# Both heads' scores on the two halves of the array's rows in four fp16 passes; P stays in PSUM and is transposed as two fp16 words by transfers; a new order

## The chip, the cores and the metric

The kernel runs on one core of one Trainium2 chip. The core has TensorE (PE, matrix products on an array of 128 rows by 128 columns, results in PSUM), VectorE (DVE), ScalarE (ACT), GpSimd (POOL), and SyncE (SP), which here issues all DMA transfers. SBUF is the on-chip memory that operands lie in; PSUM has eight banks of 512 fp32 columns by 128 partitions. The metric is the device time of one execution in microseconds.

## The reference

Attention with a forget decay over 8 batches, 8 heads, 576 positions and head size 64, then a layer with a softmax-gated activation (SoLU) and a layer norm on 4608 tokens:

```python
cum = np.cumsum(np.log(np.clip(f, 0.0001, 1.0)), axis=-1)
scores = scale * np.matmul(q, k.transpose(0, 1, 3, 2))
scores = np.where(causal, -1e9, scores + cum[:, :, :, None] - cum[:, :, None, :])
attn = np.exp(scores - np.max(scores, axis=-1, keepdims=True))
attn = attn / (np.sum(attn, axis=-1, keepdims=True) + 1e-09)
x = np.matmul(attn, v)              # to (4608, 512)
h = x @ w_in                        # (4608, 1024)
e = np.exp(h - np.max(h, axis=-1, keepdims=True))
solu = h * e / (np.sum(e, axis=-1, keepdims=True) + 1e-09)
ln = (solu - mean) / np.sqrt(var + 1e-06) * g_ln
out = ln @ w_out                    # (4608, 512)
```

The term cum of the query cancels in the softmax, so only that of the key is added. All is computed to about fp32 accuracy.

## The kernel before

**Words.** A number is held as a high and a low word, and a product of two such numbers is three matmuls: high by high, high by low, low by high. x, P (the softmax), v, the activation z and both weights are two fp16 words; q and k are two fp32r words.

**Tiling.** The work unit of attention is a pair of heads p (32 pairs, 4 in a batch). A pair has five query tiles i: 64, 128, 128, 128 and 128 queries against 64 + 128 i keys. Tiles 0 to 2 are half 0, tiles 3 and 4 half 1. The layer works on 36 blocks of 128 tokens, as soon as all the pairs of a batch's half are done. The names in the listings: `qs`, `ks`, `kz`, `qz` are q's and k's words stacked to 128 rows, `p` the scores and P, `pth`/`ptl` the transposed high and low words of P, `v` the words of v, `x_h`/`x_l` the attention's output, `hps` the two banks of x @ w_in, `z`/`zz` the activation and its transposed words, `ps`, `ps_t`, `ps_o` pools of two banks each.

**A pair.** `load` brings raw q and k by DMA. `split_qk` makes the high words (POOL, L589) and low words (POOL or DVE, L592) and copies them by DMA on SP into the stacked buffers (L339). `score_products` runs each head's scores as two fp32r passes on all 128 rows, L657 and L658; the second also adds the decay. Half 0 of batch 0 uses native fp32 instead (L655, values L774), which need no splitting. `scores`: DVE masks and reduces to the row's extreme, from PSUM to SBUF (L678); ACT takes exp with its sum (L681); DVE inverts the sum (L692, L693); POOL normalises in place (L708). `transposes`: PE transposes P square by square (L739) into `ps_t`, ACT takes the high word (L333), DVE the low one (L747). For i = 4, POOL and DVE make the words before (L703, L705) and two DMA transposes turn them (L342). `values`: transposed P by v, the first key tile on the whole array (L778), the others with each head on half of the array's columns (L782); ACT and DVE (L801, L802) write x's words.

**A layer.** L818 to L820 compute h; DVE L831 and ACT L834 the softmax; DVE L840 and following the gate; ACT L846 the squares; POOL L335 and DVE L860 the words of z. For layers 5 to 29 they are turned by two DMA transposes of 64 blocks; in others PE transposes z (L872). L888 to L890 multiply by w_out.

**What sets the order.** `Plan` is a list scheduler inside the kernel. Every operation has an engine, a cost, a due time (tables such as `DUE`, `EARLY`, `PAIR`, `AT_P`, `AT_L`) and what it reads, writes and takes from the pools. It fixes each engine's order; at run time each engine works through its list in that order and waits for semaphores. Where the plan has a gap on PE at the beginning and end of the program (`FILLED`), PE gets filler matmuls on an identity matrix, whose results are never used (L991).

Of the kernel before, what the change touches and what calls it, by code (L numbers as in the profile page):

```python
# [8 lines left out]
F32 = mybir.dt.float32  # L9
# [15 lines left out]
HALF_S = 320  # L25
MASK = -8.0e9
# [13 lines left out]
VN, VN_EARLY = 2 * NQ, 6  # L40
# [4 lines left out]
W_UP, W_TOP = (1, 1, 1, 1, 3, 3, 1, 1), (1, 1, 1, 1, 1, 1, 1, 1)  # L45
P_32, X_32 = (1, 1, 2, 1), (1, 2, 2, 1, 1, 2, 1, 2)
TURN = (450.0, 15.0, 1700.0)
FILLED = ((0.0, 140.0, 1.2), (690.0, 1000.0, 0.8))
TURNED = (5, 30)
Z_ENG = (3, 3, 1, 2)  # L50
# [4 lines left out]
SWITCH = ((0.0, 40.0, 0.0, 95.0), (0.0, 0.0, 0.0, 95.0), (0.0, 10.0, 0.0, 95.0), (130.0, 230.0, 180.0, 0.0))  # L55
# [11 lines left out]
class Plan:  # L67
# [31 lines left out]
    def schedule(self):  # L99
# [11 lines left out]
        for _ in self.ops:  # L111
# [79 lines left out]
DUE = dict(load=77.279, split=-5.82, upper=-59.07, v=-11.029, S=((-16.591, 2.389), (-10.866, -1.366), (-5.374, -8.943), (-5.783, 2.152), (-2.369, 2.528)), T=((-4.114,), (-6.578,), (0.027, -77.756), (12.862, 14.095), (-144.678, 29.668, 76.368)), V=((16.423, 371.464), (24.511, 165.955)))  # L191
EARLY = dict(load=-5.393, split=100.725, upper=-110.557, v=36.25, S=((216.478, -198.746), (23.491, -109.734), (23.153, -123.713), (-123.145, 60.456), (26.752, 113.365)), T=((-12.366,), (-36.759,), (-81.739, -143.07), (38.749, -11.206), (-229.138, -88.73, -36.262)), V=((-26.507, -137.733), (60.804, 84.836)))
PAIR = 23.079
C_OUT = 31.47
START = 86.666
HALF = ((64.967, -14.868), (32.745, -34.71))
W_IN = (-57.941, 54.591)
W_OUT = (103.025, 310.791)
LOAD = (198.891, -63.738)
WI_SCALE = (-43.671, -130.632)  # L200
VDUE = ((-38.21, -22.856, 38.942), (79.121, -21.859, -165.431), (55.69, -110.294, -55.795))
W_SCALE = 138.576
# [10 lines left out]
def tile_kernel(ctx: ExitStack, tc: tile.TileContext, qk, v, f, w_in, w_out, g_ln, out):  # L213

    nc = tc.nc  # L220

    def early(p, half):

        return p < NPAIR and half == 0
# [3 lines left out]
    plan = Plan(s=2, t=2, o=2)  # L228
# [34 lines left out]
    op(POOL, 1500, -85, masks, writes=[("mask",)])

    raw = [sb(f"raw_{n}", 2, S) for n in range(2)]
    hi = [sb(f"hi_{n}", S, dtype=F32R) for n in range(2)]

    def q32(n):
        return buf(f"{('qs', 'vs')[n // 2]}_{n % 2}", "q", 2, HALF_S)

    def k32(n):
        return buf(f"{('kz', 'ks')[n // 2]}_{n % 2}", "k", 2, HALF_S)

    def qs(p):
# [12 lines left out]
    def ptx(p, half, x):
        w = (64 + 256 * 5, 256 * 9)[half]
        if early(p, half):
            return buf(f"pt{'hl'[x]}_{half}", "f32", w)  # L290
        return buf(f"pt{'hl'[x]}_{half}", "f16", w, dtype=F16)

    nm = [sb(f"nm_{n}", NQ, 2) for n in range(2)]

    sums = [[sb(f"sm_{n}_{i}", 2 if i == 1 else 1, 2) for i in range(1, NQ)] for n in range(2)]
    inverses = [[sb(f"ri_{n}_{i}", 2 if i == 1 else 1, 2) for i in range(1, NQ)] for n in range(2)]
    sm, ri = ([[x[0][:, 0], x[0][:, 1], *(y[:, 0] for y in x[1:])] for x in xs] for xs in (sums, inverses))

    def epsilons():
        for t in sums[0] + sums[1]:  # L300
            nc.gpsimd.memset(t, 1.0)
    op(POOL, 1000, -70, epsilons, writes=[("eps",)])
# [43 lines left out]
    c_dram = nc.dram_tensor("c_scratch", [2 * B * H, 2, S], F32).ap()  # L346
    ft, zero = et[:B * H, :S], zt[:B * H, :S]
    cc = buf("pth_1", "cc", 256 * 9, dtype=F32R)[:B * H].rearrange("p (o r s) -> p o r s", o=2, r=2)
    nhalf = sb("nhalf", 1, p=B * H)
    dma(-99, ft, f.rearrange("b h s -> (b h) s"), 144, writes=[("e",)])  # L350
    op(DVE, 400, -99, lambda: nc.vector.memset(zero, 0.0), writes=[("z",)])

    for n, sl in enumerate((slice(0, HALF_S), slice(HALF_S, S))):
        op(DVE, (330, 300)[n], -99 + n, lambda sl=sl: nc.vector.tensor_scalar(ft[:, sl], ft[:, sl], 1.0e-4, 1.0, ALU.max, ALU.min),
           reads=[("e",)], writes=[("f", n)], port=True)
        op(ACT, (560, 490)[n], -99 + n, lambda sl=sl: nc.scalar.activation(ft[:, sl], ft[:, sl], AF.Ln), reads=[("e",)], writes=[("f", n)])

    op(ACT, 1500, -40, lambda: nc.scalar.activation(nhalf, ft[:, 0:1], AF.Exp), reads=[("e",), ("f", 0), ("f", 1)], writes=[("table",)])


    c32 = pt[4][:H, :2 * HALF_S]
    first = yt[:B * H, :HALF_S]
    op(DVE, 830, -99, lambda: nc.vector.tensor_tensor_scan(first, ft[:, :HALF_S], zero[:, :HALF_S], 0.0, ALU.add, ALU.add),
       reads=[("e",), ("f", 0), ("z",)], writes=[("y",)], port=True)
    op(DVE, 1380, -30, lambda: nc.vector.tensor_tensor_scan(zero, ft, zero, 0.0, ALU.add, ALU.add),
       reads=[("e",), ("f", 0), ("f", 1)], writes=[("z",)], port=True)
# [7 lines left out]
    summed = [("p", 4), ("p", 4, "c"), ("p", 4, "d")]

    for c in range(2):
        def zeros(t=qz[c]):
            nc.vector.memset(t.bitcast(F32), 0.0)
            nc.vector.memset(t.bitcast(F32)[D:D + 2], -8.0)
        op(DVE, 1000, -98, zeros, writes=[("qz", c, h) for h in range(2)])  # L380
# [19 lines left out]
    def weights(src, n, due, t, tk, w, wk, first=(), clear=()):  # L400
# [637 lines left out]
```

## Time and profile before

| | us |
|---|---|
| median of 3 runs | 762.63 (761.61 to 763.7) |
| span of the profiled execution, first to last instruction | 757.0 |
| mean granted TensorE clock | 0.998 |
| PE's first matmul | 3.41 |
| windows 0 to 72 us, PE busy | 65.25 |
| 72 to 200 us, PE busy | 119.14 |
| 600 to 683 us, PE busy | 79.87 |

The span is the profiled execution's own time from its first to its last instruction; the runs' times also hold what lies around it, 5.6 us by the median. Busy times of PE hold overlap, since a matmul is counted until its modelled end while the next has begun. A row of a group names the line, the engine, the operation, the tiles (out<-in), the shape and the count, then busy time and mean, then the idle time just before and what ended it. A row of a timeline begins with start and duration.

### The profile page before, as it was taken

The numbers are of one execution on the slowest core, as the hardware profiler recorded it, in microseconds if no ns is written. First come the engines' busy times: TensorE is split into PE (matmuls) and PEld (weight loads), VectorE is DVE, ScalarE is ACT, GpSimd is POOL, SyncE is SP. The second block draws the span as 40 slices with busy tenths as digits, with TensorE's granted clock in tenths as the row PEclk, the third lists the DMA queues.
The fourth block names the chain that finished last, engine by engine and source line by source line (L and its number), as shares of the span: only waits on it lengthen the run. The fifth ranks groups of instructions, "written<-read, shape, count | busy, mean of one in ns | idle before, by whom it ended". The sixth has DMA issues, their size and how long they took to land. (4 is left out here: it accounts for less than half of the span.)

```text
span 757.0 us, 15810 instructions
## 1 busy us (share of the span) xinstructions
PE 722.8 (95%) x4983; PEld 453.5 (60%) x4983; DVE 608.3 (80%) x1828; ACT 474.1 (63%) x1239; POOL 456.7 (60%) x645
## 2 busy tenths in 40 slices
PE   8998999988999999999999999999999999999998
PEld 7775676655656566555556666555565555554445
DVE  6557888899997899989599999999897869883343
ACT  5698977676665667755466677655565556653333
POOL 5537496656674787668377777775786666531220
PEclk9999999999999999999999999999999999999999
DMA  9557948968879898989789899889899788442001
GB/s 320 139 210 207 272 115 223 206 169 213 197 172 214 173 239 177 225 207 213 165 188 211 200 228 213 202 206 192 189 206 202 146 192 166 95 106 42 29 15 42
DMA packets 176851, 134.87 MB, mean 178 GB/s; under 512 B 128704, under 2 KB 139712, under 8 KB 175744
## 3 DMA queue, kind: packets, MB, share of 16 engines
q1 hardware_dynamic: 176768, 133.87, 75.3%
q8 instruction: 39, 0.64, 0.4%
q14 instruction: 44, 0.36, 0.2%
HBM read 39.51 MB, written 10.03 MB: 65 GB/s over the span
## 5 line engine op out<-in xcount | busy, mean ns | idle before, releaser
L681 ACT ACTIVATE p<-p,nm 128x320 f32<-128x320 f32 (+4 forms) x320 | 177.1, 554 | 88.7 <-DVE nm L678 83.4
L708 POOL TENSOR_SCALAR p<-p,ri 128x192 f32<-128x192 f32 (+4 forms) x264 | 153.2, 594 | 90.2 <-DVE ri L693 66.2
L678 DVE CUSTOM_DVE_ANT_0 p<-ps,mask 128x320 f32<-128x320 f32 (+4 forms) x320 | 126.3, 419 | 16.0 <-PE ps L658 11.2
L657 PE MATMUL ps<-ks_f32r,qs_f32r 128*128 128x448 f32 (+4 forms) x360 | 120.6, 359 | 4.6 <-DVE nm L678 3.7
L333 ACT ACTIVATE pth_f<-ps_t 128x512 f16<-128x512 f32 (+4 forms) x200 | 85.2, 442 | 46.1 <-PE ps_t L739 41.3
L818 PE MATMUL hps<-wi_h,x_h 128*128 128x512 f16 x288 | 109.9, 381 | 0.5 <-DVE e L840 0.5
L888 PE MATMUL ps_o<-wo_f,zz 128*128 128x512 f16 x280 | 106.8, 381 | 2.6 <-DMA zz<-z 2.2
L820 PE MATMUL hps<-wi_h,x_l 128*128 128x512 f16 x288 | 109.1, 379 | 0.0
L819 PE MATMUL hps<-wi_l,x_h 128*128 128x512 f16 x288 | 109.1, 379 | 0.0
L890 PE MATMUL ps_o<-wo_f,zz 128*128 128x512 f16 x280 | 106.1, 379 | 0.4 <-DVE zz L880 0.4
L889 PE MATMUL ps_o<-wo_f,zz 128*128 128x512 f16 x280 | 106.1, 379 | 0.0
L739 PE MATMUL ps_t<-ident,p 128*128 128x128 f32 x548 | 90.8, 279 | 13.1 <-DVE ptl_f L747 4.6
L658 PE MATMUL ps<-kz_f32r,qz 128*128 128x448 f32 (+4 forms) x360 | 100.8, 296 | 2.0 <-DMA kz_f32r<-c_scratch 1.2
L747 DVE TENSOR_TENSOR ptl_f<-ps_t,pth_f 128x512 f16<-128x512 f32 (+3 forms) x188 | 91.9, 502 | 8.1 <-ACT pth_f L333 7.7
L739 PEld LDWEIGHTS ps_t<-ident,p 128*128 128x128 f32 x548 | 64.4, 141 | 45.6 <-POOL p L708 13.0
L657 PEld LDWEIGHTS ps<-ks_f32r,qs_f32r 128*128 128x128 f32 (+1 forms) x360 | 64.9, 182 | 23.9 <-DVE nm L678 11.8
L589 POOL TENSOR_SCALAR hi<-raw 128x576 fp32r<-128x576 f32 (+1 forms) x64 | 48.4, 756 | 35.4 <-DMA kz_f32r<-raw 13.1
L658 PEld LDWEIGHTS ps<-kz_f32r,qz 128*128 128x128 f32 (+1 forms) x360 | 65.2, 182 | 5.1 <-issue 1.5
L850 POOL TENSOR_SCALAR st<-st 128x1 f32<-128x1 f32 x36 | 11.1, 308 | 89.0 <-ACT z L846 79.2
L703 POOL TENSOR_SCALAR wo_p<-p,ri 128x576 f16<-128x576 f32 x56 | 47.1, 851 | 27.9 <-DVE ri L693 14.8
L831 DVE TENSOR_REDUCE st<-hps 128x1 f32<-128x1024 f32 x36 | 43.9, 1218 | 21.1 <-PE hps L820 20.8
L681 ACT ACTIVATION_READ_ACCUMULATOR p<-p,nm 128x1 f32 (+1 forms) x320 | 60.1, 188 | 0.0
(194 smaller groups left out, 1416.2 us busy)
## 6 DMA issues: line engine op xcount, KB each, us to landing
raw<-in_qk_dram SPq DMA_DIRECT2D x32, 576.0 KB
ks_f32r<-hi SPq DMA_DIRECT2D x128, 144.0 KB
kz_f32r<-raw SPq DMA_DIRECT2D x64, 144.0 KB
vraw<-in_v_dram SPq DMA_DIRECT2D x28, 320.0 KB
out_dram<-y SPq DMA_DIRECT2D x35, 256.0 KB
qs_f32r<-hi SPq DMA_DIRECT2D x56, 144.0 KB
qs_f32r<-raw SPq DMA_DIRECT2D x56, 144.0 KB
qz<-hi SPq DMA_DIRECT2D x56, 80.0 KB
```

Source lines behind the costliest of these rows:

```text
L657: nc.tensor.matmul(dst, qs(p)[:, h, q0:q0 + nq], ks(p)[:, h, cols], start=True, stop=False)
L658: nc.tensor.matmul(dst, z[:, h, z0:z0 + nq], kz(p)[:, h, cols], start=False, stop=True)
L678: op(DVE, R_NS[i], at + 0.5, lambda a=a, e=e, key=key, o0=o0: nc.vector.tensor_tensor_reduce(pr[:, a:e], ps[plan.place[key]][:nq, o0:o0 + ...
L681: op(ACT, E_NS[i], at + 1.3, lambda: nc.scalar.activation(pr, pr, AF.Exp, bias=x, scale=-1.0, accum_out=sm[m][i][:nq, h:h + 1]), [("nm", m ...
L708: op(POOL, N_NS[j], at + 2.8, lambda g=g, j=j, pg=pg, r1=r1: nc.gpsimd.tensor_scalar(pg, pg, r1, 1.0, ALU.mult, ALU.mult), [("ri", m, j)], ...
L739: nc.tensor.transpose(tp[:, s, :], pt[i][:, k * P:(k + 1) * P], ident)
L818: nc.tensor.matmul(hps[:, sl], x_h, wi_h[:, c, sl], start=(c == 0), stop=False)
L819: nc.tensor.matmul(hps[:, sl], x_h, wi_l[:, c, sl], start=False, stop=False)
L820: nc.tensor.matmul(hps[:, sl], x_l, wi_h[:, c, sl], start=False, stop=(c == NCC - 1))
L888: nc.tensor.matmul(o, zz[a][:, 0, j], wo(0, k), start=(k == 0), stop=False)
L889: nc.tensor.matmul(o, zz[a][:, 0, j], wo(1, k), start=False, stop=False)
L890: nc.tensor.matmul(o, zz[a][:, 1, j], wo(0, k), start=False, stop=(k == NFC - 1))
```

## The change

- **Scores** (L614, L612): q and k are scaled to fp16 by a power of two for each batch and split into two fp16 words (`qk16`; POOL or another engine for the high word, DVE L566 for the low). A pair's heads lie on rows 0 to 63 and 64 to 127. Each score tile takes four passes (high by high, low by high, high by low, and a constant `pattern` by the decay in three bf16 words, `crow`); in each pass head 0's matmul uses the upper half of the array's rows and head 1's the lower, each into a bank of its own. The stacked copies by DMA go, and so does native fp32. ScalarE squares all of q, k and v of a batch (L485) for its scales before its q and k are split.
- **P in PSUM**: the reduce (L629) and, for i < 4, exp (L632) work in place in the bank. ACT (i < 4, L332) or POOL (i = 4, L334) writes the high fp16 word to SBUF, DVE the low one (L656).
- **Transposes**: one DMA transpose for each tile turns both words (L341, 160 in all); PE's, and L333 and L747, go. z is turned by one transfer in layers 3 to 32, and its low word is made by POOL (L751).
- **Values** (L678, L681) run per query tile, 64 or 128 moving columns; before they ran per key tile, up to 320 columns.
- **PSUM**: one pool of six banks for all but h. Four raw, `qk16` and `v16` buffers, two of e, z and y.
- **Order**: new tables. The last batch does half 0 of all its pairs first, then half 1. 761 fillers (L904) where there were 462.

Lines of the diff, removed code as above left out:

```diff
+QK = 16.0
...
+NRAW, NQK, NS = 4, 4, 6
+HOME = (1, 1, 1, 1, 0)
...
-TURNED = (5, 30)
+TURNED = (3, 33)
...
-PAIR = 23.079
+PAIR = 18.61
+FINAL = ((586.02, -122.72), (549.93, -100.91))
...
-    plan = Plan(s=2, t=2, o=2)
+    plan = Plan(s=NS)
...
+    qk16 = [sb(f"qk16_{n}", 2, 2, S, dtype=F16) for n in range(NQK)]
+    crow = sb("crow", 2, NPAIR, S, dtype=BF16)
+    pattern = sb("pattern", P, dtype=BF16)
...
+        op(ACT, 210 + n * 0.84, due, lambda: nc.scalar.activation(
+            junk[:, :n], src, AF.Square, scale=SMALL, accum_out=tops[b % 2][:, j, hp:hp + 1]),
+           [key], [("top", b % 2, hp, j)])
...
     def split_qk(p, at):
+        b, m = p // NPAIR, p % NQK
+        for j in range(2):
+            x, x16_ = raw[p % NRAW][:, j], [qk16[m][:, n, j] for n in range(2)]
+            s, sk = scales[b][:, 1, j + 1:j + 2], [("raw", p % NRAW), ("scale", b, j + 1)]
+            copied(Q_HI[p], {ACT: 720, POOL: 722, DVE: 400}, at, x16_[0], x, sk, [("qk", m, j)], scale=s)
+            op(DVE, 735, at, lambda x=x, x16_=x16_, s=s: nc.vector.scalar_tensor_tensor(x16_[1], x, s, x16_[0], ALU.mult, ALU.subtract),
+               [*sk, ("qk", m, j)], [("qkl", m, j)], port=True)
...
     def score_products(p, pieces, at):
+
+        m = p % NQK
+        keys = list(dict.fromkeys(k for h in range(2) for i, a in pieces for k in score_keys(p, i, h)))
 
         def products():
+            hi, lo = qk16[m][:, 0], qk16[m][:, 1]
+            for i, a in pieces:
                 e = cuts(i)[1 + (a > 0)]
+                q0 = q_lo(i)
+                for n, (x, y) in enumerate(((hi, hi), (lo, hi), (hi, lo), (None, None))):
+                    for h in range(2):
+                        k0 = P * (4 - i) if h == 0 else 0
+                        dst, cols = bank(p, i, h, int(a > 0))[:, :e - a], slice(k0 + a, k0 + e)
+                        if x is None:
+                            nc.tensor.matmul(dst, pattern[row(h)], crow[row(h), (p // NPAIR) % 2, p % NPAIR, cols], start=False, stop=True)
+                        else:
+                            nc.tensor.matmul(dst, x[row(h), 0, q0:q0 + P], y[row(h), 1, cols], start=(n == 0), stop=False)
+        ns = sum(4 * max(90.0, SHORT * (cuts(i)[1 + (a > 0)] - a) + 3) for i, a in pieces)
+        op(PE, ns, at, products, [*((x, m, j) for x in ("qk", "qkl") for j in range(2)), *(("crow", (p // NPAIR) % 2, h) for h in range(2)), ("pattern",)],
+           [*keys, *(("sb", *k) for k in keys), ("turn",)], take=tuple(keys), form=SCORE)
...
+        op(DVE, R_NS[i], at + STEPS[0], lambda: nc.vector.tensor_tensor_reduce(
+            whole_bank(p, i, h), whole_bank(p, i, h), cut(i, mask[:, m0:m0 + kn]), -0.125 / QK, BIG, ALU.add, ALU.min, accum_out=x),
+           [*keys, ("mask",)], [tok, ("nm", m, i, h)])
+        op(ACT, E_NS[i], at + STEPS[1], lambda: nc.scalar.activation(
+            home(), whole_bank(p, i, h), AF.Exp, bias=x, scale=-1.0, accum_out=sm[m][:, i, h:h + 1]),
+           [*keys, tok, ("nm", m, i, h), ("table",)], [*place, ("sm", m, i, h)], clear=clear)
...
+            copied(P_HI[j], {POOL: N_NS[j], ACT: 240 + 0.78 * w, DVE: 67 + 1.05 * w}, at + STEPS[3], h16, src, reads, [("p16", n2, j, g)], scale=r1, clear=prior, port=not HOME[j])
+            op(DVE, L_NS[j], at + STEPS[4], lambda h16=h16, l16=l16, src=src, r1=r1: nc.vector.scalar_tensor_tensor(l16(), src(), r1, h16(), ALU.mult, ALU.subtract),
+               [*reads, ("p16", n2, j, g)], [("p16l", n2, j, g)], port=not HOME[j], clear=prior)
...
+        turned_dma(at, lambda: turned_p(p, i).rearrange("p x s w -> p (x s) w"), lambda: p16(p, i)[:nq], nq // 16 * 2 * (2 * i + 1),
+                   [(x, m, i, h) for x in ("p16", "p16l") for h in range(2)], [("pt", m * (i < 3), i)], clear=to)
...
+        def product(i):
+            o, t = ps[:, plan.place[key]], turned_p(p, i)
+            a, n = q_lo(i) - 320 * half, q_n(i)
+            for j in range(i + 1):
+                for c, (x, y) in enumerate(((0, 0), (1, 0), (0, 1))):
+                    if j == 0:
+                        nc.tensor.matmul(o[:, a:a + n], v16[m][:, x, :2].rearrange("p t d -> p (t d)"), t[:, y, i], start=(c == 0), stop=(i == 0 and c == 2))
+                        continue
+                    for h in range(2):
+                        nc.tensor.matmul(o[row(h), a:a + n], v16[m][:, x, 2 * j + h], t[:, y, i + j if h else i - j], start=False, stop=(j == i and c == 2))
...
```

On PE, a score run between layer matmuls before, i = 2 of one pair (`ps_147` and `ps_148` are the two banks):

```order
L890 MATMUL ps_o_152<-wo_f_1181,zz_0_1_106 128x512
L657 MATMUL ps_147<-ks_f32r,qs_f32r 128x320
L658 MATMUL ps_147<-kz_f32r,qz_63 128x320
L657 MATMUL ps_148<-ks_f32r,qs_f32r 128x320
L658 MATMUL ps_148<-kz_f32r,qz_63 128x320
L739 MATMUL ps_t_151<-ident,p_65 128x128
L818 LDWEIGHTS x_h
L818 MATMUL hps<-wi_h,x_h 128x512
```

And after, i = 3 of one pair, its last passes (the two matmuls of a pass read alike; one is each head's):

```order
L614 LDWEIGHTS qk_2_71
L614 MATMUL ps<-qk_2_71 128x448
L612 LDWEIGHTS pattern
L612 MATMUL ps<-crow,pattern 128x448
L612 LDWEIGHTS pattern
L612 MATMUL ps<-crow,pattern 128x448
L710 LDWEIGHTS x_h
L710 MATMUL hps<-wi_h,x_h 128x512
```

Two long passes for each head have become four short-row ones for both, and the transposes behind them are gone.

On PE, values of half 1 before (`pth_f` and `ptl_f` are P's words, `v_0` both words of v):

```order
L778 LDWEIGHTS v_0_78
L778 MATMUL ps_o_153<-pth_f_979,v_0_78 128x256
L778 LDWEIGHTS v_0_78
L778 MATMUL ps_o_153<-pth_f_979,v_0_78 128x256
L778 LDWEIGHTS v_0_78
L778 MATMUL ps_o_153<-ptl_f_985,v_0_78 128x256
L657 MATMUL ps_148<-ks_f32r,qs_f32r 128x288
L658 MATMUL ps_148<-kz_f32r,qz_64 128x288
L657 MATMUL ps_147<-ks_f32r,qs_f32r 128x288
L658 MATMUL ps_147<-kz_f32r,qz_64 128x288
L782 LDWEIGHTS v_0_78
L782 MATMUL ps_o_153<-pth_f_979,v_0_78 64x256
```

and after, of a tile i < 3 (`t_1_p` holds both of P's words):

```order
L678 LDWEIGHTS v_1_79
L678 MATMUL ps<-t_1_p,v_1_79 128x128
L681 LDWEIGHTS v_1_79
L681 MATMUL ps<-t_1_p,v_1_79 64x128
L681 LDWEIGHTS v_1_79
L681 MATMUL ps<-t_1_p,v_1_79 64x128
```

The moving operand of these values matmuls has gone from 256 columns to 128, and each tile's run changes from the whole array to its halves.

On SP, in the middle of the program, before (`z` and `zz` are the layer's, `wo_p` the words of P for i = 4):

```order
L339 DMA kz_f32r<-raw_71 64x576
L339 DMA ks_f32r<-hi_74 64x576 x2
L339 DMA kz_f32r<-raw_71 64x576
L339 DMA qs_f32r<-hi_73 64x576 x2
L339 DMA qs_f32r<-raw_71 64x576
L339 DMA qz_63<-hi_73 64x320 x2
L339 DMA qs_f32r<-raw_71 64x576
L339 DMA kz_f32r<-c_scratch 2x2x576
L342 DMA_TRANSPOSE zz_0_0_105<-z 128x8x128
L342 DMA_TRANSPOSE zz_0_1_106<-z 128x8x128
L342 DMA_TRANSPOSE pth_f_979<-wo_p_1848 128x9x128
```

and after (`p16s` and `wo_p` hold P's words, `t_0_p` is transposed P):

```order
L341 DMA_TRANSPOSE zz_1_106<-z_104 128x16x128
L338 DMA raw_67<-in_qk_dram 128x1152
L341 DMA_TRANSPOSE t_0_p<-wo_p_1575 128x18x128
L341 DMA_TRANSPOSE t_0_p<-p16s_82 128x2x64
L341 DMA_TRANSPOSE t_0_p<-p16s_82 128x6x128
L341 DMA_TRANSPOSE t_0_p<-p16s_82 128x10x128
L341 DMA_TRANSPOSE zz_0_105<-z_103 128x16x128
L338 DMA out_dram<-y_140 128x512
L338 DMA raw_68<-in_qk_dram 128x1152
L338 DMA vraw_75<-in_v_dram 128x4x640
L341 DMA_TRANSPOSE t_0_p<-wo_p_1540 128x14x128
```

The copies of q's and k's words are gone, and transposes of P stand among raw, v, z and output transfers in one queue.

More of the change, by code (lines that the diff above doesn't have):

```diff
@@ L293, in tile_kernel @@
[L293 to L302, printed above, removed]
+    op(POOL, 1300, -65, masks, writes=[("mask",)])
@@ new lines, in tile_kernel, with rows @@
+    raw = [sb(f"raw_{n}", 2, S) for n in range(NRAW)]
+    qk16 = [sb(f"qk16_{n}", 2, 2, S, dtype=F16) for n in range(NQK)]
+    crow = sb("crow", 2, NPAIR, S, dtype=BF16)
+    pattern = sb("pattern", P, dtype=BF16)
+    def rows():
+        nc.gpsimd.memset(pattern, 0.0)
+        for r in (0, D):
+            nc.gpsimd.memset(pattern[r:r + 3], -8.0 * QK)
+    op(POOL, 500, -64, rows, writes=[("pattern",)])
+    for n in range(2):
+        op(DVE, 900, -64 + 60 * n, lambda n=n: nc.vector.memset(crow[:, n], 0.0), writes=[("crow0", n)])
@@ L358, in tile_kernel @@
[L358 to L366, printed above, removed]
@@ L374, in tile_kernel @@
[L374 to L380, printed above, removed]
-    for n in range(NPAIR):
-        op(POOL, 650, 12.0 * n - 90, lambda n=n: nc.gpsimd.memset(q32(n)[D:D + 1], -8.0), reads=summed if n else (), writes=[("one", n)])
-    pth1 = [("pth", 3), ("pth", 4)]
@@ L482, in scale @@
[L482 to L493 removed]
+                nc.vector.tensor_scalar(f, f, 2.0 ** -112, None, ALU.mult)
@@ new lines, in scores, with between @@
+        sums, r_ = (t[m][:, both[0]:i + 1].rearrange("p n g -> p (n g)") for t in (sm, ri))
+        spare = score_keys(p, i, 0)[:1]
+        other = ("sb", *spare[0])
+        def between():
+            return ps[:, plan.place[spare[0]], 508:508 + 2 * len(both)]
+        op(DVE, 70, at + STEPS[2], lambda: nc.vector.tensor_scalar(between(), sums, 1.0e-9, 1.0 / P_UP, ALU.add, ALU.mult),
+           [*spare, *(("sm", m, j, g) for j in both for g in range(2))], [other])
+        op(DVE, 82, at + STEPS[2], lambda: nc.vector.reciprocal(r_, between()), [*spare, other], [("ri", m, j) for j in both])
@@ L755, in values @@
[L755 removed]
+        m, (b, hp) = p % NQK, divmod(p, NPAIR)
+        w = (320, 256)[half]
         x0 = (b % 2) * S + 320 * half
[L757 to L782 removed]
@@ L798, in values @@
-        up = scales[0][:, 1:2] if native else 1.0 / P_UP
-        rk = [key, ("scale", 0)] if native else [key]
+        key, xk = ("s", "o", p, half), ("xt", b % 2, half, hp)
+        tiles = ((0, 1, 2), (3, 4))[half]
+        def product(i):
[6 more added lines that the diff above has]
+                        continue
+                    for h in range(2):
+                        nc.tensor.matmul(o[row(h), a:a + n], v16[m][:, x, 2 * j + h], t[:, y, i + j if h else i - j], start=False, stop=(j == i and c == 2))
@@ L800, in values @@
+        for i in tiles:
+            ns = 3 * q_n(i) * SHORT * (1 + i) + 6 * (1 + 2 * i)
+            op(PE, ns, at + 0.2 * (i - tiles[0]), lambda i=i: product(i), [("pt", p % 2 * (i < 3), i), ("v16", m), ("v16l", m)], [key],
+               take=key if i == tiles[0] else None, clear=[xk], form=HALVES if i else WHOLE)
+        up = 1.0 / P_UP
         xo = [t[:, hp, x0:x0 + w] for t in x16]
-        op(ACT, 160 + 0.9 * w, at + 1.5, lambda: nc.scalar.activation(xo[0], ps_o[plan.place[key]][:, :w], AF.Copy, scale=up), rk, [xk])
@@ new lines, in layer @@
+                op(c_eng, {DVE: 360 if last else 690, POOL: 1220}[c_eng], at, lambda sl=sl: engine(c_eng).tensor_scalar(
+                    zt[:, sl], et[:, sl], s[:, 4:5], s[:, 7:8], ALU.add, ALU.mult), [ek, ("st", n % 2), ("st7", n % 2)], [zk], clear=[zk_, (*zk_, "l")], port=c_eng == DVE)
+        at += tz - tmid + at_z
+        if turned:
+            turned_dma(at - 4.5, zz.rearrange("p a x k n -> p (a x k) n"), z16.rearrange("p a x n -> p (a x n)"), 128,
+                       [zk_, (*zk_, "l")], [(x, n % 2, a) for x in ("zh", "zl") for a in range(2)])
@@ L885, in product_out @@
+            op(ACT, 500, at + 0.5, lambda a=a, key=key: nc.scalar.copy(zz[:, a, 0], ps_t(key)), [key], zk[:1])
+            op(DVE, 683, at + 1.0, lambda a=a, key=key: nc.vector.tensor_tensor(
+                zz[:, a, 1], ps_t(key), zz[:, a, 0], ALU.subtract), [key, zk[0]], zk[1:])
+        at += 1.0 + at_out
+        key, yt, yk = ("s", "o", "y", n), yts[n % 2], ("y", n % 2)
         def product_out(k):
-            o = ps_o[plan.place[key]]
+            o = ps[:, plan.place[key]]
             a, j = divmod(k, 4)
-            nc.tensor.matmul(o, zz[a][:, 0, j], wo(0, k), start=(k == 0), stop=False)
@@ L979, in tile_kernel @@
         layers((p + 1) // NPAIR * S)
+    for half in range(2):
+        for n in range(NPAIR):
+            p = (B - 1) * NPAIR + n
+            at = FINAL[half][0] + FINAL[half][1] * n
+            if half == 0:
+                if n == 0:
+                    prepare_batch(B - 1, at)
+                whole(p, at, LATE)
+            half_of(p, half, at, LATE)
+        layers((B - 1) * S + (320, S)[half])
     blank = ident.bitcast(BF16)
```

671 lines of the change are left out of this document (264 added, 407 removed).

## Prediction

> **What bounds the kernel now.** First the page's busy times, then the windows by stage, then the waits of TensorE (PE).
>
> ```profile
> PE 722.8 (95%) x4983; PEld 453.5 (60%) x4983; DVE 608.3 (80%) x1828; ACT 474.1 (63%) x1239; POOL 456.7 (60%) x645
> 200.00:600.00 400.00, 389.65 (x2657) 236.97 (x2656) 354.88 (x1083) 253.87 (x692) 276.31 (x371) 1.00 0.90 200
> 683.00:757.00 74.00, 68.87 (x367) 35.86 (x363) 28.16 (x57) 26.70 (x45) 10.39 (x17) 1.00 0.11 28
> PE ps_t L739 <- DVE ptl_f L747: 4.6, 10, 1.0
> PE ps_o L888 <- DMA zz<-z: 2.2, 3, 1.0
> PE ps_o L778 <- DMA ptl_f<-wo_p: 1.1, 2, 0.8
> L818 PE MATMUL hps<-wi_h,x_h 128*128 128x512 f16 x288 | 109.9, 381 | 0.5 <-DVE e L840 0.5
> ```
>
> PE is busy 722.8 of 757.0 us, and 97% of the stretch from 200 to 600 us (busy columns in the order PE, PEld, DVE, ACT, POOL, then the clock, granted in full, the DMA share and GB/s). Its waits are single events of a microsecond. So PE's work sets the time, with VectorE (DVE) at 89% of that stretch and DMA at 0.90 close behind. I therefore count what the change does to PE's stream, and then ask whether others can still keep up.
>
> A busy time is no price here, since matmuls overlap: L818 lasts 381 ns by its row, but such matmuls start 0.21 us apart. I use distances between starts:
>
> ```profile
> 613.94 0.38 PE L890 MATMUL ps_o<-wo_f,zz 128*128 128x512 f16 x1
> 614.16 0.38 PE L778 MATMUL ps_o<-pth_f,v 128*128 128x256 f16 x2
> 614.38 0.27 PE L778 MATMUL ps_o<-ptl_f,v 128*128 128x256 f16 x1
> 614.58 0.41 PE L782 MATMUL ps_o<-pth_f,v 128*64 128x256 f16 x4
> 614.82 0.28 PE L782 MATMUL ps_o<-ptl_f,v 128*64 128x256 f16 x2
> 614.93 0.39 PE L782 MATMUL ps_o<-pth_f,v 128*64 128x256 f16 x4
> 615.15 0.28 PE L782 MATMUL ps_o<-ptl_f,v 128*64 128x256 f16 x2
> 615.26 0.28 PE L782 MATMUL ps_o<-pth_f,v 128*64 128x128 f16 x4
> 615.85 0.55 PE L739 MATMUL ps_t<-ident,p 128*128 128x128 f32 x3
> 616.15 0.39 PE L657 MATMUL ps<-ks_f32r,qs_f32r 128*128 128x320 f32 x1
> 616.82 0.39 PE L818 MATMUL hps<-wi_h,x_h 128*128 128x512 f16 x1
> ...
> 400.10 0.60 PE L739 MATMUL ps_t<-ident,p 128*128 128x128 f32 x4
> 400.54 0.38 PE L888 MATMUL ps_o<-wo_f,zz 128*128 128x512 f16 x1
> ```
>
> - 512 columns take 0.215 us: **0.42 ns per column**.
> - Four fp32 transposes take 0.44 us: **0.11 us each**.
> - L782, on 64 of the array's columns, runs two at a time: four matmuls of 256 columns from 614.93 to 615.15, 0.055 us each, half of 256×0.42. The 27 values matmuls from 614.16 to 615.85 take 1.69 us; by columns they come to 3×256×0.42 + (18×256 + 6×128)/2×0.42 = 0.32+1.13 = 1.45, so entering and leaving the halves costs about **0.25 us a run**.
> - The score run of four 320-column passes (616.15 to 616.82) takes 0.67, against 0.54 by columns; runs lie between that 0.13 and nothing over their columns. I take **0.05 a run**.
>
> **The change part by part.** Its own time base is the profiled execution's span, 757.0; the median of the runs, 762.63, lies 5.6 above, and I add this at the end.
>
> *P's transposes leave PE:* 548 × 0.109 = **−59.7**. z of layers 3 to 32, not only 5 to 29, now turns by DMA, so 88 PE transposes become 48: **−4.4**. The ScalarE and DVE operations behind them (L333, L747) go too, and what is late next is the transpose's landing (below).
>
> *The native fp32 scores and values of batch 0 go:*
>
> ```profile
> L774 PE MATMUL ps_o<-pth_f,vraw 64*64 64x320 f32 (+2 forms) x48 | 6.2, 377 | 0.0
> L655 PE MATMUL ps<-kz_k,qs_q 65*128 65x320 f32 (+2 forms) x24 | 5.2, 344 | 0.0
> L655 PE MATMUL ps<-ks_k,vs_q 65*128 65x320 f32 (+2 forms) x24 | 5.1, 340 | 0.0
> ```
>
> Their busy time together is **−16.5**; since matmuls overlap it is the upper end, and half of it (two of L774 at a time, on halves of the array) the lower.
>
> *Scores.* Before: 195,584 columns × 0.42 = 82.1, and 151 runs (stretches of score matmuls between others, counted in the order of instructions) × 0.05 = 7.6. After: four passes over 1,600 key columns in 32 pairs, each pass a couple of matmuls, one head on each half of the rows. If the couples run together, 204,800 × 0.42 = 86.0. No row of before shows two matmuls on halves of the rows; the nearest is L782, on halves of the columns, where two run in the time of one. The bounds of a couple are one and two matmuls' time (the second is a rival). Entering and leaving such a run costs between L657's 0.05 and L782's 0.25; I take 0.15, since the run shares the halved array with the one and whole columns with the other: 99 runs, 14.9 (bounds 5 and 25). Together **+11.2** (+1 to +21). The Trainium skill, "TensorEngine Tiling (Array Packing)", section Key Properties, says that a change of the tiling mode drains TensorE, and that tiles operate independently. L782's 0.25 and its pairs agree with both; by that rule alone the entry would be 0.25 and the sum 10 us higher, an estimate.
>
> *Values.* Before: whole-array ones (28×960 + 32×768)×0.42 = 21.6, halves 118,272×0.42 = 49.7, 60 entries × 0.25 = 15: 86.3. After, they run per query tile: 3×1,856 columns × 32 pairs × 0.42 = 74.9, but with 128 entries, 32.0: 106.9. **+20.6** (from −11, if the entries cost nothing, up).
>
> *Fillers* (L904; L991 before): the order holds 761, before 462.
>
> ```profile
> L991 PE MATMUL hps<-ident 128*128 128x256 bf16 x352 | 42.5, 278 | 3.4 <-POOL ident masks.py:199 3.4
> 71.59 0.38 PE L818 MATMUL hps<-wi_h,x_h 128*128 128x512 f16 x1
> ```
>
> 352 of before stand ahead of the first layer matmul at 71.59, in what would otherwise be a gap, and there are 584 after: at 0.42×256 = 0.109, **+25.3**. That head is longer since batch 0 now needs scales for q and k (squares of all of q and k first). The layers would then start at about 80 to 87: 71.6 + 25.3 − 16.5 is 80.4, and batch 0's scores in couples and values per tile (120 and 108 matmuls in the head) come on top; their time is in the terms above. Bounds 0 and 25.3, as the fillers might only fill what native fp32 left; I take the upper end, as each one issued has its own time on PE. The 67 others (177 against 110) stand where PE waits anyway: 0.
>
> Sum: 757.0 − 59.7 − 4.4 − 16.5 + 11.2 + 20.6 + 25.3 = 733.5, and 5.6 is **739**.
>
> *What must stay covered.* These cost nothing only if nobody makes PE wait.
>
> ```profile
> L747 DVE TENSOR_TENSOR ptl_f<-ps_t,pth_f 128x512 f16<-128x512 f32 (+3 forms) x188 | 91.9, 502 | 8.1 <-ACT pth_f L333 7.7
> L705 DVE SCALAR_TENSOR_TENSOR wo_p<-p,ri,wo_p 128x576 f16<-128x576 f32 x56 | 51.5, 947 | 0.8 <-POOL wo_p L703 0.8
> L860 DVE TENSOR_TENSOR z<-e,z 128x1024 f16<-128x1024 f32 x25 | 33.3, 1332 | 4.2 <-POOL z L335 4.2
> L592 DVE TENSOR_TENSOR raw<-raw,hi 128x576 fp32r<-128x576 f32 x28 | 25.0, 891 | 1.8 <-POOL hi L589 1.4 <-issue 0.3
> L802 DVE SCALAR_TENSOR_TENSOR x_l<-ps_o,x_h 128x256 f16<-128x256 f32 (+1 forms) x60 | 26.7, 447 | 7.3 <-ACT x_h L801 6.9
> ```
>
> DVE loses these first four groups, 201.7 us. It gains lo words (L656): 65,536 columns at L802's 447/286 = 1.56 ns (102 us), 64 of i = 4 at L705's 0.947 (61 us), and 64 of q and k at L592's 0.891 (57 us). About 220, so DVE stays near 620 us, where PE has fallen to some 700: it is the second limit. The reduce and exp in PSUM have no row; by columns they are today's operations, and the two 288-column reduces of i = 4 become one. POOL falls from 650 instructions to 348, and ScalarE gains the hi words but loses L333.
>
> On SP, the queue of all DMAs, 720 become 297, but transposes go from 106 to 190:
>
> ```profile
> q1 hardware_dynamic: 176768, 133.87, 75.3%
> 632.20:633.80 1.60, 1.60 (x9) 0.75 (x9) 1.42 (x5) 0.83 (x2) 1.18 (x2) 1.00 1.07 203
> ```
>
> From 632.20 on, one transpose of P (nine 128×128 squares) has the engines nearly to itself for 1.6 us: 0.18 us a square, 203 GB/s. Transposed bytes go from 29.6 to 67.1 MB (16,384 blocks of 4 KB), while about 52 MB of q/k copies go: 119 MB at 203 GB/s is 586 us, 80% of the span against 75.3% before. It fits on average. The Trainium skill, "VectorE: DVE Perf Modes", section The three transpose paths, gives 1309 ns to a 128×128 transpose by DMA and 390 to TensorE's. By that figure the 2,048 squares here would take 2.7 ms, an estimate; the trace, with 0.18 (369 us for all) and PE's 0.11, does not agree with either.
>
> What is new is the wait: a transpose stands at the head of SP until the tile's last lo word is made, and raw, v, out and z transfers queue behind it; raw's four buffers give three pairs of slack. On PE a score run now needs two free banks (four for i = 4) of a pool of six that also serves values and layer outputs, and P holds its banks until hi and lo words are out; layer matmuls stand behind it.
>
> **The rivals.**
> - **R2, slower: couples do not overlap.** Two matmuls on halves of the rows run one after the other. Price 86.0, giving 825. For it: no row shows row halves together. Against: L782. It decides once a couple costs over 1 + 23.6/86 = 1.27 of one.
> - **R3: new waits on PE**, for late DMA transposes or held banks. Today's two waits of values on transposed P reach 0.8 us each; once in each of 32 pairs is +26: 765. For it: DVE and DMA full at 200 to 600. Against: today's 3.3 us of such waits.
> - **R4: the others are looser.** POOL and SP issue far less, the six-bank pool lets PE choose. PE is idle for 757.0 − 722.8 = 34 us; half of it goes (−17), and score entries cost 0.05 (−10): 712.
>
> **How the numbers follow.** Forecast 0.52, R2 0.10, R3 0.21, R4 0.17. The range, 708 to 772, reaches from R4 to past R3, and leaves out R2 and some of both tails, 0.2 together. About 0.3%, 2.3 us, is what a measurement of this kernel can tell from no change. Under 760.3 lie the forecast, R4 and a small part of R3: 0.75; within 0.3% 0.05; above R2 and most of R3: 0.20.
>
> **What the profile after would show.** Right: no P transposes on PE, and couples of L614 starting two at a time, 448 columns in 0.19 us; eight such passes in some 0.9 us between layer matmuls; the first L710 at 80 to 90; PE over 94% busy from 200 to 600. Wrong: eight passes in 1.5 us (R2); PE idle over 50 us in all with L678 or L681 waiting for t tiles, or L614 for banks (R3); the first layer at 72, in which case the head's term was too large.

## The result, and the profile after

The changed kernel takes 1646.01 us (median of 4 runs, 1634.97 to 1653.87) against 763.16 before: a ratio of 2.159, 95% interval 2.148 to 2.170. The forecast was 739, the range 708 to 772. The page of the profile after, its busy times and the granted clock in 40 slices:

```profile
span 1633.2 us, 18239 instructions
PE 999.6 (61%) x6545; PEld 493.9 (30%) x6545; DVE 673.3 (41%) x1807; ACT 591.7 (36%) x1435; POOL 292.4 (18%) x343
PEclk9869576666675756765556669787687578788679
q1 hardware_dynamic: 284150, 115.14, 30.6%
```

And its window from 200 to 600 us (PE, PEld, DVE, ACT, POOL busy, clock, DMA share, GB/s):

```profile
200.00:600.00 400.00, 222.47 (x1522) 109.97 (x1522) 162.82 (x450) 136.16 (x348) 64.13 (x76) 0.66 0.30 67
```

Before, PE was 97% busy here. Now no engine is: PE 56%, DVE 41%, ScalarE 34%, DMA 0.30. Such a picture fits engines that wait for each other in turn. The span has grown by 876.2 us. PE's idle time went from 34.2 to 633.6 us (span less busy), +599; its busy time rose by 277, although by the forecast's sum PE has less to do, while the granted clock fell from 0.998 to 0.717. PE's timeline shows the waits and the slower matmuls:

```profile
805.21 0.74 PE L614 MATMUL ps<-qk 64*128 64x448 f16 x6 [1.71 <-DVE p16s L656]
805.79 0.35 PE L612 MATMUL ps<-crow,pattern 64*128 64x448 bf16 x2
807.72 0.48 PE L678 MATMUL ps<-t_p,v 128*128 128x128 f16 x3 [1.58 <-DVE st L723]
808.13 1.17 PE L681 MATMUL ps<-t_p,v 128*64 128x128 f16 x18
810.19 0.59 PE L779 MATMUL ps<-wo_f,zz 128*128 128x512 f16 x1 [0.90 <-DVE nm L629]
810.57 0.63 PE L780 MATMUL ps<-wo_f,zz 128*128 128x512 f16 x1
811.00 0.63 PE L781 MATMUL ps<-wo_f,zz 128*128 128x512 f16 x1
812.28 0.59 PE L779 MATMUL ps<-wo_f,zz 128*128 128x512 f16 x1 [0.64 <-DVE p16s L656]
812.66 0.63 PE L780 MATMUL ps<-wo_f,zz 128*128 128x512 f16 x1
813.09 0.63 PE L781 MATMUL ps<-wo_f,zz 128*128 128x512 f16 x1
815.09 0.58 PE L779 MATMUL ps<-wo_f,zz 128*128 128x512 f16 x1 [1.37 <-DVE nm L629]
```

The layer's output (L779 to L781) is one sum of 24 matmuls in one bank. Yet every third of them waits, for a reduce (L629) or a low word (L656) of a score tile, which lies in another bank of the same pool. Between such waits the matmuls start 0.38 to 0.43 us apart instead of 0.215. The waits go both ways; from the lists of PE's and of DVE's waits (total, times, longest):

```profile
PE ps L614 <- DVE p16s L656: 60.0, 22, 8.5
PE ps L779 <- ACT ps L632: 51.4, 39, 3.5
PE ps L779 <- DVE nm L629: 35.8, 32, 3.4
...
DVE ps L629 <- PE ps L781: 78.2, 42, 4.1
...
DVE ps L629 <- ACT ps L632: 55.8, 61, 3.3
```

DVE's reduce waits for layer matmuls, and PE's layer matmuls for exps and reduces. The program as built has these waits in it. Of the 280 matmuls of L779, each the first of a group of three, 194 carry a wait on another engine's semaphore; before (L888) 16 of 280 did. An excerpt of PE's program after; in brackets stands whose semaphore a matmul waits for:

```
L779 LDWEIGHTS zz_1_106
L779 MATMUL ps<-wo_f_1405,zz_1_106 128x512 [waits Activation_49]
...
L779 LDWEIGHTS zz_1_106
L779 MATMUL ps<-wo_f_1405,zz_1_106 128x512 [waits DVE_49]
```

Before, the six banks were six tiles, named `ps`, `ps_t` and `ps_o`. After, they are one: `ps = pp.tile([P, NS, 512], F32, name="ps")`. So the theory: waits are set between all accesses to a declared PSUM tile, whichever bank they touch.

### The profile page after: what moved, and what is told of

Same layout as the page of the kernel before. It is cut to its first block, busy times and chain, and to the rows that moved or that the text cites. A ratio compares the mean times of both kernels' runs of the same rounds, so it can differ in the third digit from the quotient of the medians.

```text
span 1633.2 us, 18239 instructions
## 1 busy us (share of the span) xinstructions
PE 999.6 (61%) x6545; PEld 493.9 (30%) x6545; DVE 673.3 (41%) x1807; ACT 591.7 (36%) x1435; POOL 292.4 (18%) x343
## 5 line engine op out<-in xcount | busy, mean ns | idle before, releaser
L779 PE MATMUL ps<-wo_f,zz 128*128 128x512 f16 x280 | 138.5, 495 | 233.5 <-ACT ps L632 51.4
L629 DVE CUSTOM_DVE_ANT_0 ps<-ps,mask 128x576 f32<-128x576 f32 (+4 forms) x320 | 159.8, 499 | 268.8 <-PE ps L781 78.2
L632 ACT ACTIVATE ps<-ps,nm 128x192 f32<-128x192 f32 (+3 forms) x256 | 114.8, 448 | 358.5 <-DVE nm L629 156.5
L614 PE MATMUL ps<-qk 64*128 64x288 f16 (+4 forms) x1152 | 129.0, 351 | 156.0 <-DVE p16s L656 60.0
L678 PE MATMUL ps<-t_p,v 128*128 128x128 f16 (+1 forms) x480 | 62.9, 260 | 172.5 <-DVE wo_p L656 28.3
L781 PE MATMUL ps<-wo_f,zz 128*128 128x512 f16 x280 | 145.3, 519 | 0.0
L780 PE MATMUL ps<-wo_f,zz 128*128 128x512 f16 x280 | 144.5, 516 | 0.0
L656 DVE SCALAR_TENSOR_TENSOR p16s<-ps,ri,p16s 64x64 f16<-64x64 f32 (+2 forms) x192 | 75.8, 412 | 152.4 <-ACT p16s L332 62.9
L332 ACT ACTIVATE p16s<-ps,ri 64x64 f16<-64x64 f32 (+2 forms) x192 | 75.8, 416 | 162.9 <-DVE p16s L656 45.4
L614 PEld LDWEIGHTS <-qk 64*128 64x128 f16 x1152 | 60.4, 111 | 218.9 <-issue 173.3
L678 PEld LDWEIGHTS <-v 128*128 128x128 f16 x480 | 43.5, 115 | 225.7 <-issue 189.2
L681 PE MATMUL ps<-t_p,v 128*64 128x128 f16 x1920 | 111.2, 282 | 0.0
L751 POOL TENSOR_TENSOR z<-e,z 128x1024 f16<-128x1024 f32 x30 | 65.4, 2180 | 233.3 <-ACT z L332 233.3
L334 POOL TENSOR_SCALAR wo_p<-p,ri 128x576 f16<-128x576 f32 x64 | 53.6, 849 | 283.7 <-issue 159.2
L632 ACT ACTIVATE p<-ps,nm 128x576 f32<-128x576 f32 x64 | 47.2, 739 | 149.5 <-DVE nm L629 80.1
L904 PEld LDWEIGHTS <-ident 128*128 128x128 bf16 x761 | 81.8, 110 | 59.7 <-issue 23.2
L681 PEld LDWEIGHTS <-v 128*64 128x64 f16 x1920 | 84.1, 147 | 21.0 <-issue 16.3
```

Source lines behind the costliest of these rows:

```text
L614: nc.tensor.matmul(dst, x[row(h), 0, q0:q0 + P], y[row(h), 1, cols], start=(n == 0), stop=False)
L629: op(DVE, R_NS[i], at + STEPS[0], lambda: nc.vector.tensor_tensor_reduce(whole_bank(p, i, h), whole_bank(p, i, h), cut(i, mask[:, m0:m0 + ...
L632: op(ACT, E_NS[i], at + STEPS[1], lambda: nc.scalar.activation(home(), whole_bank(p, i, h), AF.Exp, bias=x, scale=-1.0, accum_out=sm[m][:, ...
L678: nc.tensor.matmul(o[:, a:a + n], v16[m][:, x, :2].rearrange("p t d -> p (t d)"), t[:, y, i], start=(c == 0), stop=(i == 0 and c == 2))
L681: nc.tensor.matmul(o[row(h), a:a + n], v16[m][:, x, 2 * j + h], t[:, y, i + j if h else i - j], start=False, stop=(j == i and c == 2))
L779: nc.tensor.matmul(o, zz[:, a, 0, j], wo(0, k), start=(k == 0), stop=False)
```

## The experiments

**How many banks a tile holds.** Two accesses of the changed kernel span two banks, the reduce and the exp of i = 4. To be able to split the tile, a first kernel changes only that (the exp, not shown, then works in SBUF); three more then also split it. The first edit makes the plan set a new order; all four kernels with it have, as built, the same instructions in the same order on every engine.

```diff
-            whole_bank(p, i, h), whole_bank(p, i, h), cut(i, mask[:, m0:m0 + kn]), -0.125 / QK, BIG, ALU.add, ALU.min, accum_out=x),
+            for n in range(2):   # i = 4
+                op(DVE, 376, at + STEPS[0], lambda n=n: nc.vector.tensor_tensor_reduce(
+                    pr[:, 288 * n:288 * n + 288], bank(p, i, h, n)[:, :288], ..., x if n else BIG, ALU.add, ALU.min, accum_out=x),
...
-    ps = pp.tile([P, NS, 512], F32, name="ps")
+    ps = [pp.tile([P, 512], F32, name=f"ps{n}") for n in range(NS)]
```

One tile (the first edit alone): 

> Only i = 4 is changed: its reduce goes in two pieces from PSUM to SBUF and its exp works in SBUF, so that no access spans two banks; the six banks stay one tile. Theory (waits are set between all accesses to one PSUM tile, whatever the bank): nothing is gained, 1,560 to 1,700 us. Rival 1 (the access that steps over two banks makes all banks between them look used): about the time of the kernel with six tiles, 720 to 800. Rival 2 (DMA transposes are late): 1,560 to 1,700 too.

Six tiles: 

> The same edit of i = 4, and the six banks are six PSUM tiles. Theory: waits of layer matmuls on ScalarE and VectorE vanish, PE is over 90% busy, clock above 0.95, and the time comes to the recorded sum, 720 to 775 us. Rival 2 (late DMA transposes, held banks): over 1,000 us, with values matmuls waiting for DMA. Rival 3 (the clock falls with this mix of matmuls, whatever the waits): over 1,000 us at a clock near 0.7.

Two tiles: 

> The same with two tiles of three banks each. Theory: with half of the other banks in an access's own tile the false waits are fewer: between the kernel with one tile and that with six, 1,100 to 1,400 us. Rivals 1 to 3: as six tiles, or as one tile.

Three tiles: 

> The same with three tiles of two banks each. Theory: below the kernel with two tiles, 900 to 1,200 us. Rivals 1 to 3: as six tiles, or as one tile.

| tiles x banks | us | clock | PE idle (span less busy), us | waits on first matmuls of the layer's output, of 280 |
|---|---|---|---|---|
| the change: 1 x 6 | 1646.0 | 0.717 | 633.6 | 194 |
| 1 x 6, i = 4 in two pieces | 1567.9 | 0.724 | 591.4 | 174 |
| 2 x 3 | 1118.5 | 0.876 | 300.4 | 104 |
| 3 x 2 | 977.8 | 0.918 | 202.8 | 76 |
| 6 x 1 | 855.8 | 0.936 | 114.7 | 30 |

The change and the kernel with six tiles were run four times, the other three once; every step between them is larger than the 1.2% by which the runs of the change differ. The time follows the number of banks in a tile. The accesses over two banks are not the cause (Rival 1 of these runs): without them 1567.9 remain. Late transfers and the mix of matmuls (Rivals 2 and 3) are not the cause of the large loss either, since six tiles have the same transfers and matmuls. Three of the four times are where the theory put them, and so is the order of the steps. But six tiles take 855.8, ratio 1.120 (1.117 to 1.124), and not 720 to 775: something is left.

**The cause put into the kernel before.**

```diff
-    ps = [pp.tile([P, 512], F32, name=f"ps{n}") for n in range(2)]
-    ps_t = [pp.tile([P, 4, P], F32, name=f"ps_t{n}") for n in range(2)]
-    ps_o = [pp.tile([P, 512], F32, name=f"ps_o{n}") for n in range(2)]
+    banks = pp.tile([P, 6, 512], F32, name="banks")
+    ps = [banks[:, n] for n in range(2)]
+    ps_t = [banks[:, 2 + n].rearrange("p (c n) -> p c n", n=P) for n in range(2)]
+    ps_o = [banks[:, 4 + n] for n in range(2)]
```

> The kernel before, with its six small PSUM banks (two each of ps, ps_t and ps_o) declared as one tile; nothing else. Theory (waits between all accesses to one tile): it slows as the change did, 1,300 to 1,800 us, with a clock under 0.8. Rival (the slowdown needs the new scores, transfers or order): 755 to 800 us.

1346.6 us, at a clock of 0.81, a little above that expected. A row of its page and the top of PE's waits (lines have moved by one; L889 is the layer's output, L679 the reduce):

```profile
PE 951.5 (71%) x4983; PEld 529.5 (39%) x4983; DVE 610.8 (45%) x1828; ACT 492.6 (37%) x1239; POOL 431.2 (32%) x645
PE banks L889 <- DVE nm L679: 36.2, 44, 1.3
PE banks L740 <- DVE nm L679: 31.7, 33, 1.8
```

The same few lines cost the kernel before 585 us, with no other part of the change and with every engine's instructions in the old order. Of the 280 first matmuls of the layer's output 164 now carry a wait, where 16 did. With the table above, this shows the cause of the large loss.

**What is left with six tiles: the queues and buffers of transfers.** In the kernel with six tiles, PE's longest waits are for transposed P:

```profile
PE ps L688 <- DMA t_p<-wo_p: 21.3, 17, 5.3
PE hps L720 <- DVE e L742: 14.8, 8, 3.6
PE ps L614 <- DVE p16s L666: 13.9, 6, 5.5
PE ps L688 <- DMA t_p<-p16s: 11.4, 8, 3.9
```

So three kernels, each made from the one with six tiles, try the transfers: plain ones on other queues, z's transposes on PE, and a second buffer for half 1's transposed P.

```diff
 # queues (and on=nc.scalar for the two transfers to out)
-    def dma(due, out_, in_, kb, reads=(), writes=(), clear=()):
-        op(SP, kb / 0.25, due, lambda: nc.sync.dma_start(out=now(out_), in_=now(in_)), reads, writes, clear=clear)
+    def dma(due, out_, in_, kb, reads=(), writes=(), clear=(), on=None):
+        q = on or nc.gpsimd
+        op(SP, kb / 0.25, due, lambda: q.dma_start(out=now(out_), in_=now(in_)), reads, writes, clear=clear)
 # z on PE
-TURNED = (3, 33)
+TURNED = (40, 41)
 # second buffer
-NRAW, NQK, NS = 4, 4, 6
+NRAW, NQK, NS = 3, 3, 6
...
-        t = buf(f"t{half}_{p % 2 * (1 - half)}", "p", (2176, 4096)[half], dtype=F16)
+        t = buf(f"t{half}_{p % 2}", "p", (2176, 4096)[half], dtype=F16)
...
```

> Six tiles; outputs are issued on ScalarE's queue and all loads on GpSimd's, so that SP holds transposes alone. If what is left over 740 us (six tiles took 856) comes from transposes of P queued behind waiting outputs and loads: 780 to 820 us, with PE's idle time ahead of values under 20 us instead of 44. If transposes wait for P's words or buffers anyway: 840 to 880 us.

> Six tiles; all z are transposed on PE, none by DMA. If transfers are short of time: SP and DMA are freed of 30 of 190 transposes, PE's waits for values and outputs fall by 30 us or more, and despite 240 PE transposes (26 us) the time is 830 to 855 us. If not: 870 to 890 us, PE's added work on top.

> Six tiles; a second buffer of transposed P for half 1, so that a pair's transposes of tiles 3 and 4 need not wait for the values of the pair before (three raw, q/k and v buffers instead of four pay for it). If that wait at the head of SP is what holds PE: 790 to 830 us. If not: 845 to 880 us.

They take 888.4, 882.0 and 843.0 us, one run each. (The third, with its three buffers, overwrites the raw q and k of some pairs before they are used, and so computes other scores with the same kinds of instructions.) PE's waits for transposed P are 32.7 us with six tiles (the two rows above) and 42.3, 33.4 and 36.9 in these three: none of them shortens this wait. The first loses 33 us, above both branches of its expectation; its loads now stand in GpSimd's queue among GpSimd's own work. The second loses 26, where its second branch had it and about the 26 of PE's added transposes, but DVE's busy time grows too, by 24. The third gains 13, below what the wait theory asked for and a little more than the other branch allowed. In the second and third the plan also sets a new order, so these two differences are not the transfers' alone. Queues and DMA time are thus not shown to be what is left.

**What is left: the order, and which engine sets the time.** The due tables had been made for a program that reduces i = 4 in one piece. The next kernel has six tiles and new numbers in these tables; nothing else changes. Three more start from it and take work away from one engine, in the same order. (The edit of P's low words, and the zeros that fill the low words of q and k once at the start, are not shown.)

```diff
 # less DVE: low words of q and k, and of P at i = 4, on 64 columns
-nc.vector.scalar_tensor_tensor(x16_[1], x, s, x16_[0], ALU.mult, ALU.subtract)
+nc.vector.scalar_tensor_tensor(x16_[1][:, :64], x[:, :64], s, x16_[0][:, :64], ALU.mult, ALU.subtract)
...
 # less ScalarE: squares on 64 columns from batch 1 on
-junk[:, :n], src, AF.Square, scale=SMALL,
+junk[:, :n if b == 0 else 64], src if b == 0 else src[:, :64], AF.Square, scale=SMALL * (1 if b == 0 else 3.0),
 # less PE: x's low word left out of the layer
-nc.tensor.matmul(hps[:, sl], x_l, wi_h[:, c, sl], start=False, stop=(c == NCC - 1))
```

> Six tiles with other numbers in the due tables and nothing else: the tables were made for the program in which i = 4 is reduced in one piece. If what is left over the sum (856 against 739) is the order's doing: 780 to 815 us. If the order matters little: 845 to 865 us.

> The kernel with other tables, and shorter work on VectorE: the low words of q and k are made for 64 of 576 columns, and those of P at i = 4 for 64 of 576 columns from pair 4 on (the rest is left as it was). About 85 us of VectorE's 640 go; the order and PE's work stay. If VectorE, or chains through it, now set the time: 30 us or more under the kernel with other tables. If PE does: within 12 us of it.

> The kernel with other tables, and shorter work on ScalarE: the squares for the scales read 64 columns instead of 576 or 640 from batch 1 on. About 50 us of ScalarE's 557 go. If ScalarE sets the time: 20 us or more under the kernel with other tables. If not: within 10 us.

> The kernel with other tables, without the product of x's low word by w_in: 288 matmuls at 0.215 us leave PE, 62 us. If PE's work sets the time, as the prediction had it: 50 us or more under the kernel with other tables. If the other engines' chains set it: 25 us or less.

| | us | PE busy | DVE busy | ScalarE busy | PE idle |
|---|---|---|---|---|---|
| six tiles | 855.8 | 740.7 | 639.0 | 556.9 | 114.7 |
| and other tables | 803.1 | 718.6 | 638.5 | 555.6 | 82.2 |
| and less DVE work | 775.6 | 707.2 | 580.3 | 555.3 | 66.6 |
| and less ScalarE work | 803.1 | 719.0 | 639.5 | 521.3 | 82.2 |
| and less PE work | 807.5 | 682.2 | 640.5 | 555.0 | 123.5 |

Other tables gain 53 us (four runs each), so the order was about half of what was left; 803.1 is a ratio of 1.051 (1.046 to 1.056), still slower than before. The last three rows are of one run each. PE's 62 us of work may go and nothing is gained: its busy time falls by only 36, its idle time grows by 41, and the time by 4, with the clock at 0.943 against 0.972. Taking 58 us off DVE (85 had been expected) gains 27.5, just under the 30 that was asked for and well over the 12 of the other branch; taking 34 off ScalarE gains nothing. The window from 200 to 600 us, of the kernel with other tables and of the one with less PE work, shows PE giving way:

```profile
200.00:600.00 400.00, 348.80 (x3226) 177.98 (x3222) 343.21 (x1074) 292.47 (x786) 163.07 (x178) 0.95 0.74 153
...
200.00:600.00 400.00, 323.97 (x3075) 166.67 (x3076) 343.01 (x1070) 289.17 (x780) 159.73 (x176) 0.92 0.74 152
```

DVE is 86% busy in both, to a tenth of a percent, while PE's share falls from 87 to 81%. ScalarE's share is nearly the same too, 73 and 72%: such shares say only that the work goes on at the same pace. That DVE sets this pace rests on the run with less DVE work. The waits fit it; first the longest of PE in the kernel with less PE work, then those of SP's queue in the one with other tables:

```profile
PE ps L688 <- DMA t_p<-wo_p: 16.7, 14, 2.4
PE ps L688 <- DMA t_p<-p16s: 16.5, 14, 2.6
PE ps L614 <- DVE p16s L666: 12.3, 7, 4.9
...
SPq L341 <- DVE wo_p L666: 144.9, 32, 28.2
SPq L341 <- DVE p16s L666: 76.7, 26, 9.1
```

With less work of its own, PE waits longer for transposed P (33.2 us, where it was 25.7 with other tables), and the transposes stand at the head of SP's queue until DVE has made P's low words (L666). So DVE, or the chains of reduce, inverse and low word through it, most likely paces this stretch, and PE follows. Which of the two, its load or its latency, the runs do not tell apart. No kernel tried here beats the one before.

## Why the prediction was wrong

**The step that failed** is "What must stay covered. These cost nothing only if nobody makes PE wait", and in it the sentence on the pool: "a score run now needs two free banks (four for i = 4) of a pool of six". It read the six banks as six places, as the scheduler does. The built program treats them as one object, and accesses of different engines to different banks of it wait for each other. R3 had waits on PE, but priced them at 26 us from two waits of the profile before; with one tile PE's idle time grows by 599 us, and its busy time, at the lower clock, by 277. No row of the profile before could have priced it, since no tile there was shared so. The built program of the change could have shown it: a wait on 194 of 280 matmuls, where 30 are left with six tiles.

**A second step failed behind it:** "So PE's work sets the time". It held before. With PE's transposes gone and DVE's busy time at 638.5 us (608.3 before, some 620 in the prediction), 62 us less of PE's work gained nothing and 58 us less of DVE's gained 27.5: the prediction named DVE "the second limit" and gave it no price. Six tiles and other tables end 64 us above the forecast. PE's idle time is 82.2 us there, where it was 34.2 before, +48. Of the 82.2, 25.7 are waits for transposed P:

```profile
PE ps L688 <- DMA t_p<-wo_p: 18.1, 13, 2.9
PE ps L688 <- DMA t_p<-p16s: 7.6, 9, 1.3
```

That is about the size that R3 gave; and the order's share, 53 us between two sets of tables, had no place in the prediction at all.

**The terms of PE's work that the traces let one check were right**, but for a few us, as the kernels with six tiles show. Rows of the one with other tables:

```profile
307.28 0.38 PE L722 MATMUL hps<-wi_h,x_l 128*128 128x512 f16 x1
307.59 0.74 PE L614 MATMUL ps<-qk 64*128 64x448 f16 x6
308.17 0.35 PE L612 MATMUL ps<-crow,pattern 64*128 64x448 bf16 x2
308.45 0.39 PE L720 MATMUL hps<-wi_h,x_h 128*128 128x512 f16 x1
...
268.53 0.33 PE L688 MATMUL ps<-t_p,v 128*128 128x128 f16 x3
268.79 0.69 PE L691 MATMUL ps<-t_p,v 128*64 128x128 f16 x18
269.42 0.39 PE L720 MATMUL hps<-wi_h,x_h 128*128 128x512 f16 x1
```

- Couples overlap: six matmuls in 0.58 us, 0.19 a couple, as forecast; R2 does not happen. (The change itself has the same 0.58 at 805.21.)
- This score run costs 308.45 − 307.28 − 0.215 = 0.955, against 8×448×0.42/2 = 0.753 by columns: 0.20 for entering and leaving. 0.15 was taken; 99 runs make this 5 us too little. L782's 0.25 was the nearer of the two rows that bounded it. The Trainium skill, "TensorEngine Tiling (Array Packing)", section Key Properties, says that a change of the tiling mode drains TensorE; the 0.20 agrees with that.
- This values run costs 0.89 against 0.64 by columns: the 0.25 that was taken.
- The first layer matmul stands at 83.7 us with six tiles and at 87.4 with other tables, 80 to 87 forecast. In the change itself, and with one tile and i = 4 in two pieces, it stands at 129.4; the latter has the order of six tiles, so the difference is what the false waits cost.
- P's transposes by DMA are not short of DMA time on average: its share is 0.74 in the window above, and 0.30 in the change.

With other tables the span is 800.8 us, 67.3 above the sum's 733.5: 48.0 are idle time of PE and 19.3 its busy time, of which the score runs make 5. The lower clock, 0.972 for 0.998, lies in the rest; it was not measured apart. The 5.6 us that the sum adds for what lies around an execution are too many: the run with this span took 802.6 us, 1.8 more. The other 3.8 only say that the profiled execution of before was faster than its median run.

## What to carry to other kernels

In these kernels the waits that the framework set followed the declared PSUM tile and not the bank: banks that different engines use at once are better declared as separate tiles. Read the waits of the built program as well as its order before pricing a change; a wait on every third matmul of one sum is a sign of false sharing, that is, of waits between accesses that have only the declared tile in common. And once a change relieves the bound engine, sum the next one's load too: removing 62 us of PE work gained nothing here.

## What was not expected of the hardware

Short waits can be enough to lose the clock. In the kernel before with its six banks in one tile, the gaps between PE's matmuls from 200 to 600 us have a median of 0.73 us (of those over 0.1 us) and the longest is 2.5 us; the clock there is 0.76:

```profile
200.00:600.00 400.00, 272.43 (x1356) 149.01 (x1357) 181.37 (x569) 144.84 (x384) 125.17 (x188) 0.76 0.43 101
```

In the change the same window has a median gap of 1.24 us, gaps of up to 6.5 us, and a clock of 0.66. A single short gap may lose the clock or not. In the kernel with other tables, one gap of 2.31 us is followed by matmuls that start 0.38 to 0.43 us apart for 3.4 us, and one of 2.20 us by matmuls that start 0.22 us apart:

```profile
313.53 0.59 PE L789 MATMUL ps<-wo_f,zz 128*128 128x512 f16 x1 [2.31 <-DVE wo_p L666]
313.91 0.63 PE L790 MATMUL ps<-wo_f,zz 128*128 128x512 f16 x1
...
316.89 0.40 PE L791 MATMUL ps<-wo_f,zz 128*128 128x512 f16 x1
317.13 0.38 PE L789 MATMUL ps<-wo_f,zz 128*128 128x512 f16 x1
...
413.18 0.74 PE L614 MATMUL ps<-qk 64*128 64x448 f16 x6 [2.20 <-DVE ri L656]
413.75 0.37 PE L612 MATMUL ps<-crow,pattern 64*128 64x448 bf16 x2
414.05 0.39 PE L720 MATMUL hps<-wi_h,x_h 128*128 128x512 f16 x1
414.27 0.38 PE L721 MATMUL hps<-wi_l,x_h 128*128 128x512 f16 x1
```

From 317.13 on they start 0.22 us apart again. So the first of these waits cost its own time and 1.7 us more, the second its own time alone. What tells the two apart was not tested.
